# Five overlapping token tiles in place of six, in a fused attention and gated-FFN kernel

## The chip, the cores and the metric

The kernel runs on one core of a Trainium2 chip. The metric is device time in microseconds (us) of that core, as the median over runs. A timed run is about 2.1 us longer than the span of its profile (1146.01 against 1143.9 us for the kernel before); both are used below and named.

## The reference, cut to what matters

```python
# q, k, v: (batch 8, heads 8, tokens 576, 64), float32
kv  = einsum('bhsd,bhse->bhde', k, v)
out = einsum('bhsd,bhde->bhse', q, kv)
rms = sqrt(mean(out * out, axis=-1, keepdims=True) + 1e-06)
x   = out / rms * g_norm            # then reshaped to (4608 tokens, 512)
gate = 1 / (1 + exp(-(x @ w_gate)))   # w_gate, w_val: 512 x 1536
y    = (gate * (x @ w_val)) @ w_out   # w_out: 1536 x 512
```

Two heads make a pair of 128 channels, so there are 32 pairs (8 batches of 4) with 576 tokens each. For a pair, u is q times kv, x is u after the norm, and x must be transposed (channels on partitions, tokens along the free side) to feed the FFN.

## The kernel before: what the change and the argument touch

A pair is a list of small steps. Tokens are cut into six tiles of 96; `NP` is 96, `JH` is 3, `P` is 128, `HD` is 64.

```python
def q_mm():      # q transposed: six tiles of 96 tokens
    ...
def u_mm():
    ps = at_ps("u")
    d["u"] = ps[0:NP, :, 0:JH * P]
    for j in range(NJ):
        c0 = P * (j % JH)
        nc.tensor.matmul(ps[0:NP, j // JH, c0:c0 + P],
                         d["qT"][:, j // JH, NP * (j % JH):NP * (j % JH) + NP],   # stationary: 96 tokens
                         kvs[n % 2], start=True, stop=True)                       # moving: 128 columns
def u_square():  ...  # ScalarE: sq = u * u, PSUM to SBUF
def u_sum():     ...  # VectorE: sums over 64 elements
def u_root():    ...  # ScalarE: sqrt(mean + eps)
def u_norm():    ...  # VectorE: reciprocal, then u * (1 / rms) into sq
def x_mm():      ...  # TensorE: six transposes of 96 tokens
def x_out():     ...  # ScalarE: copies to xT, times g_norm
```

The first eight pairs run in a staged start, while k, v and q stream in:

```python
def stage(i, n_convert):
    do(i, KV, Q, KV_OUT, Q_OUT)
    do(i - 2, U_SUM, U_ROOT, U_NORM)
    do(i - 1, U, U_SQUARE)
    do(i - 3, X, X_OUT)
```

The first layer of the FFN begins after the last stage; I call the start of its first matmul the gate. The other 24 pairs are fed one step at a time into slots between FFN matmuls, with two empty slots before the transposes:

```python
def feed(b, at_ps):
    for n in range(NHP * b, NHP * b + NHP):
        steps = attention(n, at_ps)
        fill.extend(steps[:-2] + [lambda: None] * 2 + steps[-2:])
```

## Time and profile before

| | before |
|---|---|
| median time | 1145.19 us (6 runs, 1144.22 to 1146.63) |
| profiled span | 1143.9 us |
| TensorE busy | 1118.9 us, 98% |
| gate (first L378 matmul) | 45.80 us |
| from the gate to the end | 1098.1 us |
| u matmuls, records | 384 in 32 pairs, 12 a pair |

TensorE is busy from the gate to the end, so the span is TensorE's work plus what it waits for. Before the gate TensorE also waits for loads. The lines that carry this are in the prediction and are explained there.

### The profile page before, as it was taken

How to read it: one execution, taken by the hardware profiler on the slowest of the kernel's cores; microseconds unless marked ns; L12 is line 12 of the kernel's file. 1: busy time of each engine (PE TensorE's matmuls, PEld its weight loads, DVE VectorE, ACT ScalarE, POOL GpSimd, SP SyncE). 2: the span in 40 equal slices, each digit the busy share in tenths (PEclk: the TensorE clock that was granted, in tenths of full speed). 3: DMA queues.
4: the chain of work that ended last, by engine and by line, in shares of the span. 5: the costliest groups of instructions: out<-in, count | busy, mean ns of one | idle time of the engine just before them, and what ended most of it. 6: DMA issues, size and time to landing. Idle time of an engine off the chain costs nothing.

```text
span 1143.9 us, 14818 instructions
## 1 busy us (share of the span) xinstructions
PE 1118.9 (98%) x5712; PEld 891.6 (78%) x5712; DVE 583.7 (51%) x1121; ACT 296.2 (26%) x571; POOL 241.6 (21%) x342
## 2 busy tenths in 40 slices
PE   5899999999999999999999999999999999999998
PEld 4644444547888888888888888888888888888887
DVE  4699995054155525563365425552556246615641
ACT  3622221223133303331233213330333112101110
POOL 0000001000034303340143103430343025404420
PEclk9999999999999999999999999999999999999999
DMA  9843430211211111111111121111110000000001
GB/s 226 202 146 118 141 110 26 56 49 32 63 37 32 32 28 41 40 45 30 50 32 32 41 59 32 32 32 31 42 49 11 19 19 1 1 19 19 1 1 37
DMA packets 71589, 57.58 MB, mean 50 GB/s; under 512 B 40800, under 2 KB 65376, under 8 KB 71520
## 3 DMA queue, kind: packets, MB, share of 16 engines
q1 hardware_dynamic: 71360, 56.64, 18.5%
q8 instruction: 46, 0.75, 0.3%
q14 instruction: 23, 0.19, 0.1%
q10 hardware_dynamic: 160, 0.00, 0.0%
HBM read 47.19 MB, written 9.44 MB: 50 GB/s over the span
## 4 chain that ended last, share of the span: by engine, by line
PE 93%; DMA 3%; DVE 2%; ACT 1%; issue 1%; SPq 0%; DVEq 0%; ACTq 0%
PE mm L507 44%; PE mm L587 25%; PE two L378 10%; PE mm L363 4%; PE at L378 3%; DMA q<-in_q_dram 3%; PE at L252 3%; PE at L223 2%; PE at L278 1%; PE at L237 1%; PE mm L378 1%; ACT xT L288 0%; DVE sq L270 0%; DVE ms L261 0%; DVE sg L535 0%
## 5 line engine op out<-in xcount | busy, mean ns | idle before, releaser
L493 POOL TENSOR_TENSOR tw<-gv 128x256 f32<-128x256 f32 x168 | 120.3, 726 | 851.4 <-PE mm L507 661.6
L507 PE MATMUL mm<-xT,tw 128*128 128x256 f32 x672 | 160.1, 381 | 2.4 <-DVE gv L519 2.4
L507 PE MATMUL mm<-sx,tw 128*128 128x256 f32 x672 | 159.6, 380 | 0.0
L507 PE MATMUL mm<-xT,gv 128*128 128x256 f32 x672 | 159.4, 380 | 0.0
L507 PEld LDWEIGHTS mm<-xT,tw 128*128 128x128 f32 x672 | 124.9, 190 | 20.1 <-issue 4.2
L507 PEld LDWEIGHTS mm<-xT,gv 128*128 128x128 f32 x672 | 126.9, 190 | 17.2
L507 PEld LDWEIGHTS mm<-sx,tw 128*128 128x128 f32 x672 | 126.1, 190 | 16.7
L493 POOL TENSOR_TENSOR tw<-gv,tw 128x256 f32<-128x256 f32 x168 | 125.7, 769 | 0.0
L378 PE MATMUL two<-xT,gv 128*128 128x512 f32 x256 | 111.1, 593 | 0.5 <-DVE sq L270 0.5
L378 PEld LDWEIGHTS two<-xT,gv 128*128 128x128 f32 x256 | 48.4, 190 | 60.4 <-issue 60.2
L587 PE MATMUL mm<-w,s 128*128 128x256 f32 x384 | 89.1, 379 | 0.0
L587 PE MATMUL mm<-w,gv 128*128 128x256 f32 x384 | 88.3, 379 | 0.0
L587 PE MATMUL mm<-t2w,gv 128*128 128x256 f32 x384 | 88.1, 379 | 0.0
L536 ACT ACTIVATE sg<-sg 128x256 f32<-128x256 f32 x84 | 35.0, 416 | 187.9 <-DVE sg L535 187.3
L527 DVE TENSOR_TENSOR gv<-mm,sg 128x256 f32<-128x256 f32 x84 | 35.7, 424 | 88.9 <-PE mm L507 88.9
L587 PEld LDWEIGHTS mm<-t2w,gv 128*128 128x128 f32 x384 | 73.0, 190 | 9.9
L587 PEld LDWEIGHTS mm<-w,s 128*128 128x128 f32 x384 | 72.6, 190 | 9.7
L587 PEld LDWEIGHTS mm<-w,gv 128*128 128x128 f32 x384 | 72.5, 190 | 9.6
L507 PE MATMUL mm<-sx,gv 128*128 128x256 f32 x336 | 79.9, 381 | 0.0
L507 PEld LDWEIGHTS mm<-sx,gv 128*128 128x128 f32 x336 | 63.4, 190 | 8.8
L514 ACT COPY sg<-mm 128x256 f32<-128x256 f32 x84 | 31.3, 372 | 146.1 <-PE mm L507 146.1
L543 DVE TENSOR_TENSOR gv<-gv,sg 128x512 f32<-128x512 f32 x84 | 68.9, 859 | 0.2
(94 smaller groups left out, 1194.3 us busy)
## 6 DMA issues: line engine op xcount, KB each, us to landing
k<-in_k_dram SPq DMA_DIRECT2D x32, 288.0 KB, 3.3
v<-in_v_dram SPq DMA_DIRECT2D x32, 288.0 KB, 3.9
q<-in_q_dram SPq DMA_DIRECT2D x64, 144.0 KB, 3.1
st<-in_moe_w_gate_dram SPq DMA_DIRECT2D x12, 512.0 KB, 3.7
st<-in_moe_w_val_dram SPq DMA_DIRECT2D x12, 512.0 KB, 4.8
st<-in_moe_w_out_dram SPq DMA_DIRECT2D x12, 512.0 KB, 4.1
out_dram<-sg SPq DMA_DIRECT2D x24, 192.0 KB, 2.3
out_dram<-sg SPq DMA_DIRECT2D x24, 128.0 KB, 2.3
```

The source lines that it names most:

```text
L223: nc.tensor.matmul(ps[HD * e:HD * e + HD, 0, 0:HD], pairs[n]["k"][:, e, js], pairs[n]["v"][:, e, js], start=(j == 0), stop=(j == NJ - 1))
L237: nc.tensor.transpose(ps[:, j // JH, c0:c0 + NP], pairs[n]["q"][:, j].rearrange("p e d -> p (e d)"), ident[0:NP, 0:NP])
L252: nc.tensor.matmul(ps[0:NP, j // JH, c0:c0 + P], d["qT"][:, j // JH, NP * (j % JH):NP * (j % JH) + NP], kvs[n % 2], start=True, stop=True)
L363: nc.tensor.matmul(ps, gv[c, f][:, P * t:P * t + P], w["wo", f], start=(f == 0), stop=(f == NFT - 1))
L378: nc.tensor.matmul(self.ps[i], w[("wg", "wv")[i], self.f][:, m, :], xT[self.c][:, m, :], start=(m == 0), stop=(m == NMT - 1), skip_group_c ...
L493: nc.gpsimd.tensor_tensor(out=tw[f, i], in0=b[in0], in1=b[in1] if isinstance(in1, tuple) else tw[f, in1], op=ALU.subtract)
L507: nc.tensor.matmul(ps, wt[:, m, :], xs[:, m, :], start=(new and m == 0), stop=(m == NK - 1), skip_group_check=True)
L514: nc.scalar.copy(out=d["sg"][:, h2], in_=pa)
L527: tt(out=d["h"][:, h2], in0=pb, in1=d["sg"][:, h2], op=ALU.add)
L536: nc.scalar.activation(out=d["sg"][:, h2], in_=d["sg"][:, h2], func=AF.Sigmoid)
L543: tt(out=d["h"], in0=d["h"], in1=d["sg"], op=ALU.mult)
L587: nc.tensor.matmul(ps, hs(f), ws[:, f, :], start=(new and f == 0), stop=(f == NF2 - 1), skip_group_check=True)
```

## The change

The intent is to do less on TensorE for u. A u matmul has two operands: the tokens of qT, which weight loads (LDWEIGHTS, PEld in the profile) put into TensorE and which are called stationary, and the 128 columns of kv that move past them. In this kernel it costs what the moving operand costs: its records step by 109 ns with 96 tokens and with 116, and by 111 with 128 (experiment 7). Five tiles are enough for 576 tokens if a tile holds 116. The tiles start 115 tokens apart, so that neighbours share one token, which is computed twice and gives the same number. Square, sum and norm then handle 5 x 128 elements on 116 partitions in place of 6 x 128 on 96. The transposes drop the doubled tokens.

```diff
+    NU = 5
+    M = S // NU                 # 115
+    MU = S - M * (NU - 1)       # 116
+    UC = 192                    # columns from one u tile to the next in PSUM
+    UX = M * 3
 ...
         def u_mm():
             ps = at_ps("u")
-            d["u"] = ps[0:NP, :, 0:JH * P]
-            for j in range(NJ):
-                c0 = P * (j % JH)
-                nc.tensor.matmul(ps[0:NP, j // JH, c0:c0 + P], d["qT"][:, j // JH, NP * (j % JH):NP * (j % JH) + NP],
-                                 kvs[n % 2], start=True, stop=True)
+            d["u"] = ps[0:MU].rearrange("p i c -> p (i c)")[:, 0:NU * UC].rearrange("p (i c) -> p i c", c=UC)[:, :, 0:P]
+            qT = d["qT"].rearrange("p i n -> p (i n)")
+            for i in range(NU):
+                nc.tensor.matmul(d["u"][:, i], qT[:, M * i:M * i + MU], kvs[n % 2], start=True, stop=True)
         def u_square():
-            d["sq"] = sb.tile([NP, 2, JH * P], FP32, tag="sq", name="sq")
+            d["sq"] = sb.tile([MU, NU, P], FP32, tag="sq", name="sq")
 ...                              # u_sum, u_root, u_norm: the same with the new shapes
         def x_mm():
             d["x"] = ps = at_ps("x")
-            for j in range(NJ):
-                c0 = NP * (j % JH)
-                nc.tensor.transpose(ps[:, j // JH, c0:c0 + NP], d["xn"][:, j // JH, P * (j % JH):P * (j % JH) + P],
-                                    ident[0:NP, 0:NP])
+            for i in range(NU):
+                m_ = MU if i == NU - 1 else M
+                bank, c0 = divmod(M * i, UX)
+                nc.tensor.transpose(ps[:, bank, c0:c0 + m_], d["xn"][0:m_, i, :], ident[0:m_, 0:m_])
 ...                              # x_out: pieces split at 345 in place of 288
```

More of the change, by code (lines that the diff above doesn't have):

```diff
@@ L248, in u_mm @@
             ps = at_ps("u")
-            d["u"] = ps[0:NP, :, 0:JH * P]
-            for j in range(NJ):
-                c0 = P * (j % JH)
-                nc.tensor.matmul(ps[0:NP, j // JH, c0:c0 + P], d["qT"][:, j // JH, NP * (j % JH):NP * (j % JH) + NP],
-                                 kvs[n % 2], start=True, stop=True)
+            d["u"] = ps[0:MU].rearrange("p i c -> p (i c)")[:, 0:NU * UC].rearrange("p (i c) -> p i c", c=UC)[:, :, 0:P]
+            qT = d["qT"].rearrange("p i n -> p (i n)")
+            for i in range(NU):
+                nc.tensor.matmul(d["u"][:, i], qT[:, M * i:M * i + MU], kvs[n % 2], start=True, stop=True)
         def u_square():
-            d["sq"] = sb.tile([NP, 2, JH * P], FP32, tag="sq", name="sq")
+            d["sq"] = sb.tile([MU, NU, P], FP32, tag="sq", name="sq")
             nc.scalar.activation(out=d["sq"], in_=d["u"], func=AF.Square)
         def u_sum():
-            d["ms"] = sb.tile([NP, 2, 2 * JH], FP32, tag="ms", name="ms")
-            nc.vector.tensor_reduce(out=d["ms"].rearrange("p i n -> p (i n)"),
-                                    in_=d["sq"].rearrange("p i (n d) -> p (i n) d", d=HD), axis=AX.X, op=ALU.add)
+            d["ms"] = sb.tile([MU, NU, 2], FP32, tag="ms", name="ms")
+            nc.vector.tensor_reduce(out=d["ms"].rearrange("p i e -> p (i e)"),
+                                    in_=d["sq"].rearrange("p i (e d) -> p (i e) d", d=HD), axis=AX.X, op=ALU.add)
         def u_root():
-            nc.scalar.activation(out=d["ms"], in_=d["ms"], func=AF.Sqrt, bias=eps[0:NP], scale=1.0 / HD)
+            nc.scalar.activation(out=d["ms"], in_=d["ms"], func=AF.Sqrt, bias=eps[0:MU], scale=1.0 / HD)
         def u_norm():
@@ L269, in u_norm @@
             d["xn"] = d["sq"]
-            nc.vector.tensor_tensor(out=d["xn"].rearrange("p i (n d) -> p i n d", d=HD),
-                                    in0=d["u"].rearrange("p i (n d) -> p i n d", d=HD),
-                                    in1=d["ms"].unsqueeze(3).to_broadcast([NP, 2, 2 * JH, HD]), op=ALU.mult)
+            nc.vector.tensor_tensor(out=d["xn"].rearrange("p i (e d) -> p i e d", d=HD),
+                                    in0=d["u"].rearrange("p i (e d) -> p i e d", d=HD),
+                                    in1=d["ms"].unsqueeze(3).to_broadcast([MU, NU, 2, HD]), op=ALU.mult)
         def x_mm():
             d["x"] = ps = at_ps("x")
-            for j in range(NJ):
-                c0 = NP * (j % JH)
-                nc.tensor.transpose(ps[:, j // JH, c0:c0 + NP], d["xn"][:, j // JH, P * (j % JH):P * (j % JH) + P],
-                                    ident[0:NP, 0:NP])
+            for i in range(NU):
+                m_ = MU if i == NU - 1 else M
+                bank, c0 = divmod(M * i, UX)
+                nc.tensor.transpose(ps[:, bank, c0:c0 + m_], d["xn"][0:m_, i, :], ident[0:m_, 0:m_])
         def x_out():
@@ L285, in x_out @@
                 c, o = divmod(S * b + s0, G)
-                i, r = divmod(s0, S // 2)
-                n_ = min(G - o, S // 2 - r)
+                i, r = divmod(s0, UX)
+                n_ = min(G - o, (UX if i == 0 else S - UX) - r)
                 nc.scalar.activation(out=chunk(c)[:, m, o:o + n_], in_=d["x"][:, i, r:r + n_], func=AF.Copy, scale=g_col)
```

## The prediction

> **What bounds the kernel now.** I read first the page's busy shares and slices, to see which engine fills the span; then the chain that ended last, in order of time, to see where the six-tile steps lie on it; then the groups by shape; and last who waited for whom, to see where the shorter steps on the other engines could end a TensorE wait. Page, parts 1 and 2:
>
> ```profile
> PE 1118.9 (98%) x5712; PEld 891.6 (78%) x5712; DVE 583.7 (51%) x1121; ACT 296.2 (26%) x571; POOL 241.6 (21%) x342
> PE   5899999999999999999999999999999999999998
> PEclk9999999999999999999999999999999999999999
> DMA  9843430211211111111111121111110000000001
> ```
>
> TensorE is the bound from about 50 us to the end, at full clock. Only the first two slices (57 us) differ: there PE is not full and the DMA share is 9 and 8. What is removed from TensorE after 50 us comes off the span one for one, unless a wait stands behind it. The chain, at the start and in one feed of a pair:
>
> ```profile
> 31.28 7.98 DMA q<-in_q_dram
> 39.39 0.70 PE at L237 x6
> 40.61 0.96 DVE ms L261
> 42.18 0.95 DVE sq L270
> 43.14 0.87 DVE ms L261
> 44.70 0.97 DVE sq L270
> 45.80 3.67 PE two L378 x8
> 49.47 0.50 PE two L278 x6
> ...
> 315.76 1.31 PE at L252 x12
> ```
>
> Until 39.3 us the chain is four q loads of 8 to 9 us each, end to end: the eight pairs before that run beside transfers. From there to 45.80 it goes twice through sum (L261), root and norm (L270). Afterwards a pair appears as 12 TensorE records of L252 (u), 1.31 us, with no gap. The groups that change:
>
> ```profile
> L252 PE MATMUL at<-kv,qT 128*96 128x128 f32 x288 | 35.4, 273 | 0.0
> L252 PEld LDWEIGHTS at<-kv,qT 128*96 128x96 f32 x288 | 34.0, 163 | 3.6 <-issue 2.0
> L261 DVE TENSOR_REDUCE ms<-sq 96x12 f32<-96x768 f32 x32 | 30.2, 943 | 34.4 <-ACT sq L257 34.2
> L270 DVE TENSOR_TENSOR sq<-at,ms 96x768 f32<-96x768 f32 x24 | 22.9, 954 | 1.0
> L278 PE MATMUL at<-ident,sq 96*128 96x96 f32 x156 | 17.2, 246 | 2.2 <-DVE sq L270 2.2
> ```
>
> The mean of a matmul record (273 ns) is a latency, and records overlap; the cost is the step from one start to the next, 1.31/12 = 109 ns. There are two records per u matmul (288 records for 24 pairs of six), one per transpose.
>
> TensorE's waits that the norm's steps could shorten:
>
> ```profile
> PE mm L507 <- DVE gv L519: 2.4, 5, 0.5
> PE at L278 <- DVE sq L270: 2.2, 2, 1.6
> PE two L378 <- DVE sq L270: 0.5, 1, 0.5
> ```
>
> **What the Trainium skill says.** "TensorE: Matmul & The Clock Gate", section "Back-to-back issue gap", gives N/2.4 + 2.5 ns a pass for N moving columns at full clock; "FP8 and Floating Point Precision", section "TensorE Precision Notes", has true FP32 as four passes. A u matmul would be 4 x 128/2.4 = 213 ns plus small change; the trace has 2 x 109 = 218, so it agrees, and the cost follows the moving columns (kv, 128) and not the tokens, which are the stationary columns. "TensorE: Matmul & The Clock Gate", section "LDWEIGHTS (loading the stationary operand)", has the load growing as P/1.2 ns with P stationary columns: the trace agrees in slope, 190 ns for 128 columns against 163 for 96, 27 ns for 32. For 116 columns I estimate 163 + 20/1.2 = 180 ns, of which 116/1.2 = 97 ns is the part that can't overlap the next load; that is still under 109, so it stays behind the matmul. "VectorE: DVE Perf Modes", section on the TRN2 errata, has fp32 tensor_tensor at (N+151)/0.96 ns: for 768 that is 957, and the norm measures 954.
>
> **The change, part by part.** Every one of 32 pairs now has five u matmuls of 116 tokens (M = 115 apart, so neighbours share a token) in place of six of 96. A comparison of the two built programs, not run, shows the same order of instructions and the same waits on every engine; only shapes and counts differ. DMA work is the same.
>
> 1. u on TensorE: 12 records become 10 of the same 109 ns, 0.218 us less per pair. Eight pairs lie before 46 us beside transfers and give nothing here. Of the 24 later ones, 22 have TensorE with no wait behind the norm that could swallow it: 22 x 0.218 = 4.80 us.
> 2. Transposes of x: six of 96 moving columns take 0.50 us in the chain at 49.47, 82 ns each. From 82 at 96 columns and 109 at 128, 115 columns should take 98 and 116 take 99: 4 x 98 + 99 = 491 ns against 492. Nothing. The total of moved columns is 576 either way, because the transposes drop the doubled tokens. A small gain lies after them: the next weight load can't keep up with an 82 ns transpose (the first matmul of L507 after one takes 245 ns to the next start in the raw starts, against 216), and against a 99 ns one it lags by 17 ns less. 24 x 0.017 = 0.4 us.
> 3. Vector and Scalar: 640 elements in place of 768. At 0.96 per ns that is 133 ns less per sum (to about 810) and per norm (to about 821). Square: copies of 256 and 512 columns on ScalarE take 372 and 586 ns, 0.836 ns a column, so 802 becomes 802 - 107 = 695. Root and reciprocal barely change. The copies to xT move the same 576 columns in three pieces each time, as before. In sum some 4.3 + 4.3 + 3.4 us of engine time, nearly all beside TensorE work.
> 4. What of it is on the path. (a) Start: two sums and two norms between 40.61 and 45.66, 4 x 0.133 = 0.53 us. (b) The five waits of L507 for L519, once in each of five rounds: the raw starts show 854 ns to the next matmul in place of 216. VectorE runs L543, L573 to L576, reciprocal, norm, L519 without a gap before it, but that run begins with an L540 that waited for TensorE after the sum. So only the norm counts: 5 x 0.133 = 0.67 us. (c) The two waits of L278 for the norm, near 254 and 268 us, belong to the two pairs left out in 1. At 254 the VectorE queue is solid from 242.8, so 0.133 + 0.133 = 0.27 is gained and the 0.218 of u is lost. At 268 the chain is u, square, a table load that hides the sum, root, norm: 0.218 + 0.107 + 0.133 = 0.46, within the 0.71 us by which TensorE is late there.
>
> Sum: 4.80 + 0.40 + 0.53 + 0.67 + 0.27 + 0.46 = 7.1 us. 1146.07 - 7.1 = 1139.0 us, 0.6% less.
>
> **The rivals.** First, transposes or loads that dislike the new shape: 115 moving columns is odd, output columns start at 115, 230, and token slices start 460 bytes apart. If a 115-column transpose cost 110 ns in place of 98, the pairs after 46 us lose 24 x 5 x 12 ns = 1.4 us, and the time is 1140.4. If the 116-column load can't hide and sets a pitch of 120 ns, u gains only 12 x 109 - 10 x 120 = 108 ns per pair and the time is about 1141.4. Against both: the load of 128 columns in transposes already keeps an 82 ns pitch, and the u load has 12 ns to spare. Second, transposes bound by their number and not their columns (six loads of 128 columns become five): then another 24 x 0.082 = 2 us goes and the time is 1137. Against it: 82 and 109 ns follow 96 and 128 moving columns with no floor. Third, the start is not bound by transfers but by the loop of TensorE, VectorE and ScalarE (stages 3.3 us apart between 28 and 38 us): then each stage loses up to 0.4 us and another 2 us goes. Against it: the chain there is the q loads, and issues by the DMA queue follow each other without a pause. Fourth, a wait that moves: the x copies hold kv of the next pair back by 0.25 us in five places; they follow TensorE's own last matmuls, so they shift with it and stay.
>
> **Range and chances.** The parts that I trust most give 4.8, the others are each under a microsecond; the rivals move the sum by +2.4 or -4. The three runs of before spread over 2.4 us, which is a third of the gain. So 1139.0, from 1136.0 to 1142.0. 2% would be 23 us, over three times the whole sum; faster by over 2% gets 0.01, slower 0.01.
>
> **What would show it right or wrong.** In the changed profile: u as x10 in the chain with 1.09 us; 240 records for the later 24 pairs; the load near 180 ns; transposes of x with 0.49 us for five; sum near 810 and norm near 821 ns; the waits for L519 still five but about 0.13 shorter each; the first gate matmul near 45.3 us; q loads landing at 39.3 as before. A pitch of u over 109 ns, transposes over 99 ns, or a new wait in the x copies would make me wrong upwards; a start that ends much before 45 us, downwards.

## More of the kernel before

All runs are on a single core; every run was marked fast, and the profiled ones had a mean granted TensorE clock of 0.998 to 1.000. That mean hides the start: in all 13 profiles TensorE runs at half clock at first (the records of u step by up to 217 ns in place of 109) and reaches the full clock between 16.6 and 23.9 us.

## The result, and the profile after

The changed kernel took 1137.05 us (median of 6 runs, 1135.78 to 1138.14) against 1145.19 us. The ratio is 0.9927, with a 95% interval of 0.9914 to 0.9940. A ratio is the mean time of one kernel's runs over that of the other's of the same rounds, so it is not quite the ratio of the medians. By the 2% rule this is "same", though the gain is clear of noise.

Line numbers move: u is L259 (was L252), sum L267 (L261), norm L276 (L270), transposes of x L285 (L278), first layer L384 and L513 (L378 and L507), and the waited-for addition L525 (L519).

The first two parts of the page of the changed kernel:

```profile
PE 1112.3 (98%) x5616; PEld 885.6 (78%) x5616; DVE 575.4 (51%) x1121; ACT 293.2 (26%) x571; POOL 241.7 (21%) x342
PE   5999999999999999999999999999999999999998
```

There are 96 TensorE records fewer: 64 for u (two a pair) and 32 for the transposes (one a pair). TensorE is still the bound. The chain that ended last, in order of time (start, length, what):

```profile
29.86 7.23 DMA q<-in_q_dram
37.22 0.70 PE at L244 x6
38.43 0.83 DVE ms L267
39.88 0.82 DVE sq L276
40.70 0.74 DVE ms L267
42.12 0.84 DVE sq L276
43.09 3.67 PE two L384 x8
46.76 0.50 PE two L285 x5
...
198.70 1.09 PE at L259 x10
```

Ten u records take 1.09 us, 109 ns each as before. Five transposes take 0.50 us, as six did. The norm's chain at the end of the start, from the last q transposes to the gate, is 5.87 us (37.22 to 43.09) against 6.41 (39.39 to 45.80). But the last q load also landed 2.2 us earlier, which was not expected. The groups by shape (count, busy us, mean ns, idle before):

```profile
L259 PEld LDWEIGHTS at<-kv,qT 128*116 128x116 f32 x240 | 29.6, 180 | 3.2 <-issue 2.0
L267 DVE TENSOR_REDUCE ms<-sq 116x10 f32<-116x640 f32 x32 | 26.1, 814 | 31.8 <-ACT sq L263 31.6
L276 DVE TENSOR_TENSOR sq<-at,ms 116x640 f32<-116x640 f32 x24 | 19.8, 824 | 1.0
L263 ACT ACTIVATE sq<-at 116x640 f32<-116x640 f32 x24 | 16.8, 701 | 25.2 <-PE at L259 25.2
```

The weight load is 17 ns longer and stays behind the matmul; the steps of the norm are 129, 130 and 101 ns shorter. TensorE's waits (total us, times, longest):

```profile
PE mm L513 <- DVE gv L525: 1.7, 5, 0.3
PE at L285 <- DVE sq L276: 1.9, 2, 1.6
PE two L384 <- DVE sq L276: 0.4, 1, 0.4
```

The five waits for the addition behind the norm went from 2.4 to 1.7 us; none is new.

The profiled spans differ by 9.4 us (1143.9 and 1134.5), the medians by 8.1. Cutting both profiles at the gate shows where: before it 2.7 us (45.80 and 43.09), after it 6.7 us (1098.1 and 1091.4). The part after the gate is nearly what was predicted. The part before is too large for the 0.53 us of the prediction, so that is where the experiments had to look. A first hint that the 2.7 us are not all the change: the second pair's q transposes began at 13.89 us in place of 15.35, when no changed instruction had run yet.

### The profile page after: what moved, and what is told of

Its sections match the earlier page's. It is cut to its first block, busy times and chain, and to the rows that moved or that the text cites. A ratio compares the mean times of both kernels' runs of the same rounds, so it can differ in the third digit from the quotient of the medians. Undisturbed runs are those within 1.5% of the kernel's fastest.

```text
span 1134.5 us, 14626 instructions
## 1 busy us (share of the span) xinstructions
PE 1112.3 (98%) x5616; PEld 885.6 (78%) x5616; DVE 575.4 (51%) x1121; ACT 293.2 (26%) x571; POOL 241.7 (21%) x342
## 4 chain that ended last, share of the span: by engine, by line
PE 93%; DMA 3%; DVE 2%; ACT 1%; issue 1%; SPq 1%; DVEq 0%; ACTq 0%
PE mm L513 44%; PE mm L593 26%; PE two L384 10%; PE mm L369 4%; PE at L384 3%; PE at L259 2%; PE at L230 2%; DMA q<-in_q_dram 1%; PE at L285 1%; PE at L244 1%; PE mm L384 1%; DMA v<-in_v_dram 1%; DMA st<-in_moe_w_val_dram 1%; ACT xT L294 0%; SPq L92 0%
## 5 line engine op out<-in xcount | busy, mean ns | idle before, releaser
L513 PE MATMUL mm<-xT,tw 128*128 128x256 f32 x672 | 159.9, 381 | 1.7 <-DVE gv L525 1.7
L513 PE MATMUL mm<-sx,tw 128*128 128x256 f32 x672 | 159.5, 380 | 0.0
L513 PE MATMUL mm<-xT,gv 128*128 128x256 f32 x672 | 159.4, 380 | 0.0
L513 PEld LDWEIGHTS mm<-xT,gv 128*128 128x128 f32 x672 | 126.9, 190 | 17.2
L513 PEld LDWEIGHTS mm<-xT,tw 128*128 128x128 f32 x672 | 124.9, 190 | 19.4 <-issue 3.6
L513 PEld LDWEIGHTS mm<-sx,tw 128*128 128x128 f32 x672 | 126.1, 190 | 16.7
L384 PE MATMUL two<-xT,gv 128*128 128x512 f32 x256 | 111.1, 592 | 0.4 <-DVE sq L276 0.4
L384 PEld LDWEIGHTS two<-xT,gv 128*128 128x128 f32 x256 | 48.4, 190 | 60.4 <-issue 60.2
L513 PE MATMUL mm<-sx,gv 128*128 128x256 f32 x336 | 79.9, 381 | 0.0
L513 PEld LDWEIGHTS mm<-sx,gv 128*128 128x128 f32 x336 | 63.4, 190 | 8.8
```

The lines of the kernel that those rows point to most:

```text
L384: nc.tensor.matmul(self.ps[i], w[("wg", "wv")[i], self.f][:, m, :], xT[self.c][:, m, :], start=(m == 0), stop=(m == NMT - 1), skip_group_c ...
L513: nc.tensor.matmul(ps, wt[:, m, :], xs[:, m, :], start=(new and m == 0), stop=(m == NK - 1), skip_group_check=True)
```

## The experiments

All kernels below gave correct results. They ran in three groups (1 to 4, 5 to 8, and 9 to 11 by their labels), each on one chip beside runs of the kernel before, whose medians were 1145.12, 1144.20 and 1145.01 us. One fact made small effects readable. The time from the gate to the end repeats: 1091.39 to 1091.47 us in seven profiles whose late part is that of the changed kernel, and 1098.06 or 1098.07 in three whose late part is that of before. In the profiles nearly all of the scatter therefore lies before the gate, and I take it that the same holds for runs without one.

### 1 and 2: the change in one part only

The first kernel has five tiles in the 24 late pairs, the second in the eight early ones. Both definitions stand side by side:

```diff
+        if n >= NE:          # e2 and e9: n < NE     (NE is 8)
             def u_mm(): ...  # and the other steps, in five tiles
+        else:
+            def u_mm(): ...  # and the other steps, in six tiles
```

> Five tiles only in the 24 pairs after the start; the first eight pairs keep six tiles. From the first gate matmul to the end the two profiles differ by 6.7 us (1098.1 against 1091.4). My theory (after the start, what is taken off TensorE and the two waits comes off one for one): 6.6 to 6.7 us less than before, ratio 0.9942. A rival that puts over 2 us of the gain into the start: ratio 0.996 or more.

Measured: 1138.79 us, ratio 0.9947 (0.9934 to 0.9960), with runs from 1137.02 to 1142.37. From gate to end the profile has 1091.46 us, 6.61 less than before, as expected. The wide scatter lies before the gate, which was at 46.83 us in the profile.

> Five tiles only in the first eight pairs. My theory (the start waits for transfers, only two sums and two norms at its end are on the path): 0.5 us less than before, ratio 0.9995, and the step from the last q transposes to the first gate matmul 0.5 us shorter than the 6.4 us of before. Rival (the loop of the engines sets the start): 1.5 to 2.7 us less, ratio 0.9976 to 0.9987, with q transposes of the last early pair earlier by as much.

Measured: 1144.12 us, ratio 0.9989 (0.9977 to 1.0001). The step from the last q transposes to the gate was 5.87 us, 0.54 shorter, as expected, and the time after the gate was 1098.07 us, that of before to the digit. (The step repeats: 6.40 to 6.43 us in the three profiles with six tiles at the start, 5.86 or 5.87 in the seven with five.) The last q transposes came at 38.06 us and not 39.39, the rival's sign, but this mark scatters by more than that. The mean gain was 1.25 us: between the two expectations, and not settled by this run.

### 3: six u matmuls with the short norm

```diff
-            for i in range(NU):
+            for i in [*range(NU), NU - 1]:
```

> The changed kernel with its last u matmul done twice in every pair: TensorE has six u matmuls again, the steps of the norm stay short. My theory (0.218 us per pair, one for one, in 23 of 24 late pairs): 5.0 us over the changed kernel, near 1142 us, ratio to before 0.9972. Rival (the gain comes from the shorter norm and the waits): under 2 us over the changed kernel, ratio 0.9945 or less.

Measured: 1142.79 us, ratio 0.9983 (0.9970 to 0.9996). From the gate to the end it took 1096.45 us, 5.04 over the changed kernel; 5.0 was expected. The u matmuls count one for one on TensorE, and the rival falls. Its profile also showed something new before the gate. The chain that ended last of this kernel:

```profile
23.89 2.84 PE two L259 x12
...
30.91 0.85 PE at L230 x24
31.75 0.65 PE at L244 x6
32.40 1.33 PE two L259 x12
33.73 0.50 PE two L285 x5
34.23 0.85 PE at L230 x24
```

Here the early stages are on TensorE's own work, back to back: kv 0.85, q 0.65, u 1.33, x 0.50, 3.32 us a stage, and no load in the chain from 13.3 us to the gate. In the profile of before, the same stretch was four q loads. The first kernel of this group, which has six tiles at the start, had the same TensorE chain from 26 us on. A caution: both chains begin in a stretch of 3.4 us in which the granted clock fell back to half (from 23.9 us here, from 26.3 in experiment 1), so that the u above took 2.84 us and not 1.33. The only other profile with such a stretch is that of the changed kernel (from 23.4 us). The two profiles of a six-tile start without one, before and experiment 10, come to the last q transposes through loads. So at 3.32 us a stage, that TensorE set the last stages may be the fall of the clock; no run separates the two.

### 4 and 6: more u matmuls in the early pairs

```diff
-            for i in range(NU):
+            for i in [*range(NU)] + [NU - 1] * (2 if n < NE - 2 else 0):     # e6: 4 in place of 2
```

> The changed kernel with two more u matmuls (0.436 us) in each of the first six pairs. My theory (transfers set the start): within 0.4 us of the changed kernel, ratio to before about 0.993. Rival (TensorE or the loop of the engines sets the start): 6 x 0.436 = 2.6 us more, ratio 0.9952.

Measured: 1138.34 us, ratio 0.9940 (0.9928 to 0.9952), against 0.9927 for the changed kernel in its own rounds. The mean gate, worked out as time less 2.1 us less the time after the gate, is 44.9 us; over all runs with five tiles in the start it is 44.1 (43.8 in experiment 2, the only such start on the same chip). So 2.6 us of added TensorE work cost some 0.8 to 1.1: neither free nor one for one.

> The changed kernel with four more u matmuls (0.872 us) in each of the first six pairs, which makes a stage of TensorE's loop 3.97 us. Revised theory (TensorE's loop and the transfers are nearly equal at the start, and the longer sets it): the loop now sets every stage, some five stages x 0.436 = 2.2 us over the kernel with two more (1138.4), near 1140.6 us. Rival (transfers alone set the start): still 1138.4 or less.

Measured: 1139.57 us, ratio 0.9958 (0.9945 to 0.9972), mean gate 46.3 us, with 5.2 us of added work. Doubling the dose added 1.5 us to the gate (44.9 to 46.3, on two chips), less than the expected 2.2. The chain of this kernel shows that TensorE sets the stages now:

```profile
32.28 0.85 PE at L230 x24
33.12 0.64 PE at L244 x6
33.77 1.98 PE two L259 x18
35.75 0.50 PE two L285 x5
```

A stage is 3.97 us, as foreseen, at full clock from 20 us on. The rival that transfers alone set the start falls. With five tiles (3.10 us a stage) the chain comes to the last q transposes through loads in all seven profiles, with six (3.32) in two of three, and with seven and nine u matmuls it is TensorE's.

### 5: the changed kernel again

> The changed kernel unchanged, as the control of this group: 1137.0 us within 0.7, and from the first gate matmul to the end 1091.4 us. The spread of its runs lies before the gate. If five tiles take TensorE's loop (3.10 us a stage) clear below the transfers, its chain at the start runs through loads, as in the two profiles with five tiles so far.

Measured: 1138.39 us, ratio 0.9946 (0.9933 to 0.9958), twice the 0.7 us away that I had allowed; 1091.39 us after the gate, as expected. The same kernel was at 0.9927 in its first rounds. The chain at the start ran through loads, with the last q transposes at 38.23 us and not 37.22:

```profile
22.20 8.28 DMA q<-in_q_dram
30.49 7.60 DMA q<-in_q_dram
38.23 0.70 PE at L244 x6
```

So a good part of the first result's 2.7 us before the gate was one lucky start.

### 7: tiles of 128 tokens

```diff
-    M = S // NU
+    M = 112
```

> Five tiles of 128 tokens, 112 apart, in place of 116. My theory (the weight load hides behind the 109 ns matmul so long as its own step of about 110 ns is no longer): at most 0.3 us more, 1091.4 to 1091.7 us after the gate. Rival (the load's length of 190 in place of 180 ns shows in each of 240 records): 2.4 us more.

Measured: 1138.96 us, ratio 0.9949 (0.9937 to 0.9962), the same as the changed kernel of that group; 1091.70 us after the gate, 0.3 over it. Neighbours now share 16 tokens. The group of the weight loads in this kernel:

```profile
L259 PEld LDWEIGHTS at<-kv,qT 128*128 128x128 f32 x240 | 30.6, 192 | 2.9 <-issue 1.9
```

The load is 12 ns longer than that of 116 columns, in 240 records 2.9 us if it showed; 0.3 us showed. It is not quite hidden: from start to start the u records take 111.4 ns on average in place of 109.2, 0.54 us over 240, and the first matmuls after the transposes give 0.25 back. So the number of tokens in a tile is nearly free up to 128, and 116 is worth 0.3 us over 128.

### 8: a fourteenth slot

This one is for use. The five waits for L525 come where a norm falls between the sums at the end of one round of the first layer and the next addition on VectorE. With 13 slots a pair and 7 slots a round, the second pair of each batch meets that place. One empty slot more makes each pair two whole rounds.

```diff
-            fill.extend(steps[:-2] + [lambda: None] * 2 + steps[-2:])
+            fill.extend(steps[:-2] + [lambda: None] * 2 + steps[-2:] + [lambda: None] * (1 if b > 2 else 0))
```

> The changed kernel with one empty slot after each late pair (from the fourth batch on), so that a pair takes 14 slots, two rounds of the first layer, and every norm falls one slot later than the place where it held TensorE. If the five waits for the norm (0.50 us) and five longer waits of kv for the copies of x (0.24 us over the others) come from the place in the order: 3.7 us less, 1133.3 us, 1087.7 us after the gate. Rival (the norm holds TensorE wherever it is put): no change, 1137 us, or new waits in other places.

Measured: 1133.04 us (4 runs, 1131.94 to 1135.21), ratio 0.9902 (0.9889 to 0.9916), beside 0.9946 for the changed kernel of the same group. From gate to end it took 1087.32 us, 4.1 less than the changed kernel, where 3.7 were expected. TensorE's waits for loads and other engines, all over 0.3 us in total:

```profile
PE two L230 <- DMA v<-in_v_dram: 5.3, 1, 5.3
PE at L230 <- DMA v<-in_v_dram: 4.1, 1, 4.1
PE two L259 <- DVE sq L276: 2.7, 2, 1.3
PE at L285 <- DVE sq L276: 1.9, 2, 1.6
PE at L244 <- DMA q<-in_q_dram: 1.0, 2, 0.5
PE two L384 <- DVE sq L276: 0.4, 1, 0.4
```

The line of L513 waiting for L525 is gone, and so is that of kv waiting for the copies of x (0.9 us in the changed kernel). By the starts of the records the first were worth 2.5 us and the second 1.2; the other 0.4 us was not traced. It beats both kernels.

### 9, 10 and 11: the start once more

The second kernel's interval still reached 1.0, so the two halves and the whole were timed again beside each other.

> Five tiles only in the first eight pairs, a second time, because the first gave 1.2 us with an interval that reaches zero. Start set by transfers: 0.5 us less than before, 1144.3 to 1144.7 us. If five tiles also free the start from TensorE's loop: 1.2 to 1.7 us less.

Measured: 1143.89 us, ratio 0.9989 (0.9977 to 1.0002), a mean gain of 1.26 us.

> Five tiles only in the 24 late pairs, a second time. Start set by transfers: 6.7 us less than before, and 0.5 us over the changed kernel of this group. If the start's loop counts: still 6.7 us less than before, but 1.2 us or more over the changed kernel.

Measured: 1138.08 us, ratio 0.9938 (0.9925 to 0.9950), 7.2 us less than before in the mean, and 0.5 us over the changed kernel.

> The changed kernel, control of this group: 7.2 us less than before if the start adds 0.5 us to the 6.7 us after the gate, 8 us or more if its loop counts; 1091.4 us after the gate.

Measured: 1137.55 us, ratio 0.9932 (0.9918 to 0.9945), a mean gain of 7.6 us; 1091.43 us after the gate.

The late half alone points to 0.5 us for the start, the early half alone to 1.26. Together: the gate of every run, worked out as in experiment 4, has a mean of 44.94 us in 46 runs with six tiles at the start (before, 1 and 10), and 44.09 us in 35 runs with five (the changed kernel, 2, 5, 7, 8, 9 and 11). The difference is 0.85 us, with a standard error of 0.22 (0.15 and 0.16 us for the two means) if all runs are independent. They are not quite: group by group (the first result, then the three groups of experiments) the difference is 1.7, 1.5, -0.3 and 0.9 us, and by these four the standard error is 0.4. Single runs lie between 42.3 and 48.8 us. The sum 6.7 + 0.85 = 7.5 fits the means of all runs of the two kernels, largely the same runs: 1145.06 us in 35 and 1137.59 in 16.

The traces allow a sharper cut, made afterwards. Up to the second pair's q transposes no changed instruction has run, and there the profiles are already 3.2 us apart (13.65 to 16.86 us). From there to the gate the three profiles with six tiles at the start take 30.45, 29.97 and 30.20 us, and the seven with five take 28.32 to 29.59, 28.94 in the mean. The difference is 1.27 us, with a standard error of 0.21, and no two profiles of the two kinds overlap. So the start gives more than 0.54 us. Where the rest comes from, the chain of experiment 10 suggests: before it enters the last two q loads at 21.67 us, it goes through the first two u steps, 2.56 (at half clock) and 1.31 us, which with five tiles are 2.17 and 1.11 (experiment 9), 0.59 us less. Not every chain goes this way (that of before runs through loads from 6.18 us on), so this share of the cause is argued and not shown.

## Why the prediction was right, and where it was not

1137.05 us lies in the range 1136 to 1142, and the cause was the one named. Step by step:

- **u on TensorE: right.** The prediction had 4.80 us in 22 pairs, and 5.0 with the pair near 268 us. Putting the matmuls back cost 5.04 us after the gate. The step of a record stayed at 109 ns with a 180 ns load, as estimated, and experiment 7 shows that even 192 ns stays hidden but for 2 ns a record. The prediction's reason was less good than its result. It took 116/1.2 = 97 ns as the part of a load that cannot overlap the next; for 128 columns that gives 107 ns, under the 109 of a record, yet the records then stepped by 111.4, so there were fewer than its "12 ns to spare". And the loads of transposes that it set against this rival take 140 ns where those of u with 128 columns take 192: they are no guide.
- **Transposes: right.** Five took 0.50 us where six had; 115 columns step by 98 ns. The last one, of 116, took 103 ns in place of the 99 foreseen. The lag of the weight load after it fell from some 29 ns to 10. In the starts of the records the lag gave 0.49 us and the transposes cost 0.05, net 0.44 against 0.40: 26 pairs have their transposes after the gate, and not 24.
- **Waits of L513 for L525: right.** In the starts of the records the step is 717 ns in place of 854, 5 x 0.137 = 0.69 us against 0.67. Experiment 8 shows that these waits belong to the place of the norm in the order: with the place moved, they are gone.
- **The two pairs left out: right.** Near 254 us TensorE's lateness fell from 1808 to 1762 ns and the u matmuls by 218, together 0.26 us against 0.27. Near 268 us lateness fell by 241 ns and u by 218, 0.46 against 0.46.
- **Sum after the gate:** 4.80 + 0.44 + 0.69 + 0.26 + 0.46 = 6.65 us of the 6.66 measured.
- **The norm's chain before the gate: right.** 6.41 to 5.87 us is 0.54, against 0.53.
- **The start: a size off.** "Eight pairs lie before 46 us beside transfers and give nothing here" is the step that failed, and with it the line against the third rival. That line trusted one profile's chain. The chain of experiment 10, with the same six-tile start, goes through the first two u steps before it reaches the last loads; that of experiment 1 runs the later stages through TensorE, though after a fall of the clock; and experiments 4 and 6 show TensorE's loop and the transfers close enough that a longer stage takes over. The start gained 0.85 us over all runs (standard error 0.2 to 0.4) and 1.27 us by the cut of the profiles (standard error 0.21), in place of 0.53. The 0.54 of the norm's chain is shown; the surplus is there in the profiles, and that it comes from TensorE's shorter u steps is argued.
- **"q loads landing at 39.3 as before": wrong as a mark.** The last q transposes began anywhere from 36.61 (experiment 8) to 40.40 us (experiment 1) in the profiles whose start is that of one of the two kernels. This scatter is also most of why the time was 1137.05 for 1139.0: the prediction began from 1146.07, and all 35 runs of before have a mean of 1145.06, 1.0 us lower, while the gain over all runs was 7.5 for 7.1.

What stays open is why one start is faster than another at equal code. Most of the difference is there by the second pair's q transposes; the moved rate from 5 to 10 us ranges from 275 to 304 GB/s in the profiles of before, the changed kernel and experiments 1, 2 and 5, and nothing here varied it. The fall of the clock is not what makes the averages: with five tiles, 11 runs at a mean clock of 0.998 and 21 at 1.000 have mean gates of 44.1 and 44.0 us.

## What to carry to other kernels

For small matmuls in full fp32, count moving columns: making stationary tiles wider so that there are fewer of them saved the whole moving pass of each tile dropped here (0.218 us a pair), and doubling some rows to get there was free while the weight loads did not set the step: 109 ns a record at 116 columns, 111 at 128. Where an extra engine's step is fed into a tight loop, look at which place of the loop's order it meets: a slot more a pair gave 4.1 us here, over half of what the change itself gave. Cut profiles at a point after which times repeat; a stretch that waits for transfers needs several profiles before its chain is called the bound, and a look at the clock of that stretch, which the mean of the run hides.

## What the Trainium skill lacked or had wrong

- "TensorE: Matmul & The Clock Gate", section "LDWEIGHTS (loading the stationary operand)": the slope of P/1.2 holds (163, 180, 190 to 192 ns for 96, 116 and 128 columns), but the lengths in a trace carry some 83 ns more (190 less 128/1.2), and the page does not say how long a load stays hidden. Here fp32 records of 128 moving columns step by 109.2 ns with loads of 180 ns and by 111.4 ns with loads of 192.
- The same page, section "Part 4: PE-mode transpose": it has some 390 ns for a 128x128 bf16 transpose in isolation and 275 in a kernel, and says that the full clock does not engage for them. fp32 transposes of 96 and 115 columns last 246 and 262 ns and step by 82 and 98 ns among matmuls at full clock, but those of 115 columns by 192 in the half-clock stretch of experiment 3, so they follow the clock. Their weight loads take 141 ns for 128 columns in place of 190; the page gives no figure for either.
- "VectorE: DVE Perf Modes", section on the TRN2 errata: (N+151)/0.96 gives 824 ns for the norm of 640 elements, and 824 was measured, with a PSUM operand. For sums along the free side no figure is given; 943 and 814 ns for 768 and 640 elements fit (N+139)/0.96 within 3 ns. The ScalarE row for PSUM sources, (172+N)/1.2, gives 783 and 677 ns for the squares, which measured 802 and 701.
- No page has the scatter of a start that streams loads: the gate, worked out for the 35 runs with five tiles at the start, spread with a standard deviation of 1.0 us.
